# An attention and MLP kernel on one core: the second tile of x loaded from SP's queue, and head 0's wq issued behind the activation table load

## The chip, the cores and the metric

The kernel runs on one core of one Trainium2 chip. The metric is the device time of one execution in microseconds (us). The time of an execution is about 1.8 us more than the span of its profile (1238.05 against 1236.3 us in the profiled execution of the kernel before). A ratio of two kernels is the mean time of one kernel's fast runs over that of the other's of the same rounds, so it is not quite the ratio of the medians quoted.

## The reference

```python
x  = A_x                                   # 1 x 2048 x 512, bf16
xn = layernorm(x)
q  = (xn @ wq) as 32 heads of 128
p  = softmax(q @ k_cache^T / sqrt(128))    # 2048 keys a head
s  = (p @ v_cache) @ wo
h  = relu(xn @ w1 + b1) ** 2
g  = silu(h @ w2 + b2)
out = x + s * g
```

## The kernel before

Five engines run their own instruction lists; a helper adds the semaphore waits. TensorE (PE) takes its list strictly in order. The list begins with 36 warm-up matmuls on zeros. Head 0 has a start of its own: its keys come in two halves by plain loads, are transposed on PE and copied to SBUF by ACT, while the first tile of x is normalized on DVE and POOL, transposed on PE, copied by DVE and projected with head 0's wq.

The loads, as they stand in the program before:

```python
ln_load(0, 0, SP)          # x tile 0, 128 rows of 1 KB
ln_load(0, 1, AC)          # x tile 1
load_k0(0)                 # first half of head 0's keys, 128 rows of 2 KB, on SP
fill_wq(0, AC)             # head 0's wq, 512 rows of 256 B
load_k0(1)                 # second half of the keys, on SP
E(AC, partial(_act, out=th_t[:, 0, 0:1], in_=warm[:, 0:1], func=ACT.Exp), deps=[t_warm])
ln_load(0, 2, SP)
ln_load(0, 3, SP)
fill_wq(1)                 # head 1's wq, on SP
load_v0(0)
load_v0(1)
# ... cut: head 1's keys and values, w1
```

The order in which PE gets its first work:

```python
warm_up(36)
k0_transpose(0)            # PE: 8 transposes of the first keys
k0_copy(0)                 # ACT
ln_bn(0, 0)                # DVE: statistics of x tile 0
ln_rstd(0, 0, eng=DV)
ln_bn(0, 1)
ln_scale(0, 0)
first_transpose(0)         # PE: 4 transposes of x tile 0
k0_transpose(1)            # PE: 8 transposes of the second keys
k0_copy(1)                 # ACT
t_kfill[0] = t_k0[1]
ln_rstd(0, 1, eng=DV)
first_copy(0)              # DVE
first_proj(0)              # PE: first projection, needs wq
bias_rows()                # PE
ln_scale(0, 1)
first_evac(0)
bias_copy()
first_transpose(1)         # PE
gen_scores(0)              # PE, and exp on ACT
# ... cut
```

The transposes of the second keys stand before the first projection.

The softmax here doesn't subtract the row's maximum and nothing guards it: scores larger than these inputs give would overflow.

## Time and profile before

| kernel before | value |
|---|---|
| time, median of 6 runs | 1237.94 us (1237.75 to 1238.45) |
| span of the profiled execution | 1236.3 us |
| PE busy | 1231.7 us |
| ACT, DVE, POOL busy | 1053.5, 472.8, 31.9 us |
| first keys landed | 5.20 us |
| second keys landed | 1.67 + 4.3 = 6.0 us (issue and time to landing in the DMA view) |
| first projection on PE | 7.02 us |

PE is busy almost throughout, and the prediction shows why only the first 8 us are open to this change. The start in the view of the chain that ended last, where each line is a start, a duration in us and what took it:

```profile
1.18 4.02 DMA kT<-in_A_k_cache_dram
5.20 0.05 issue
5.24 0.94 PE psO L196 x8
6.19 0.24 PE psF L196 x4
...
7.02 0.38 PE psF L152 x4
```

The chain enters PE with the landing of the first keys at 5.20. `PE psO L196 x8` are eight key transposes, `PE psF L196 x4` the four x transposes, and `PE psF L152 x4` is the first projection.

### The profile page before, as it was taken

Reading aid. Unit: us, or ns where it says so; the run is one execution under the profiler, and the core shown is the slowest. Engines: PE = TensorE matmul, PEld = TensorE weight load, DVE = VectorE, ACT = ScalarE, POOL = GpSimd, SP = SyncE. Lnnn points to the kernel's source line nnn. Section 1 sums busy time; section 2 is a strip of 40 time slices with the busy share of each in tenths; the row PEclk is TensorE's granted clock in tenths of the full one; section 3 lists DMA queues with packets and bytes.
Section 4 is the critical chain, followed back from the end, with each engine's and each line's share of the span. In section 5 each row is a group of like instructions: output and inputs, shape, how many; then the busy total and the mean of one; then the engine's idle time right before and its main releaser. Section 6 shows DMA issues by size and latency. Waiting matters only on the chain.

```text
span 1236.3 us, 26934 instructions
## 1 busy us (share of the span) xinstructions
PE 1231.7 (100%) x11885; PEld 818.8 (66%) x11885; DVE 472.8 (38%) x953; ACT 1053.5 (85%) x1044; POOL 31.9 (3%) x73
## 2 busy tenths in 40 slices
PE   9999999999999999999999999999999999999999
PEld 7666666666666666666666666666666666666665
DVE  4453323244435332334444532333344333324333
ACT  7888888888888888888888888888888888888885
POOL 1010000000002000000000200000000000000000
PEclk9999999999999999999999999999999999999999
DMA  9999998777879897778778878787788789878771
GB/s 211 203 231 209 185 178 134 130 144 143 139 152 172 141 161 129 139 139 145 133 133 170 172 138 143 141 148 134 133 146 148 146 154 158 137 134 146 145 123 31
DMA packets 686868, 185.41 MB, mean 150 GB/s; under 512 B 673536, under 2 KB 685568, under 8 KB 686752
## 3 DMA queue, kind: packets, MB, share of 16 engines
q1 hardware_dynamic: 684656, 179.62, 80.4%
q0 software_dynamic: 1424, 3.81, 1.2%
q8 instruction: 94, 1.54, 0.6%
q10 hardware_dynamic: 672, 0.26, 0.1%
q14 instruction: 22, 0.18, 0.1%
HBM read 96.60 MB, written 2.10 MB: 80 GB/s over the span
## 4 chain that ended last, share of the span: by engine, by line
PE 99%; DMA 0%; DVE 0%; issue 0%; SPq 0%; DVEq 0%
PE psO L157 38%; PE psA L152 36%; PE psF L152 25%; DMA kT<-in_A_k_cache_dram 0%; PE psA L157 0%; DVE out_t L165 0%; PE psF L196 0%; DVE tmp_t L175 0%; PE psO L196 0%; PE psO L152 0%; DVE xnT L179 0%; SPq L208 0%; PE psA L196 0%; DVEq L119 0%
## 5 line engine op out<-in xcount | busy, mean ns | idle before, releaser
L161 ACT ACTIVATE pT<-psA 128x1024 bf16<-128x1024 f32 x1024 | 1043.5, 1023 | 163.5 <-PE psA L152 118.1
L157 PEld LDWEIGHTS psO<-v_sb,pT 128*128 128x128 bf16 x8192 | 547.7, 98 | 240.5 <-issue 12.5
L157 PE MATMUL psO<-v_sb,pT 128*128 128x129 bf16 x8192 | 631.6, 220 | 0.0
L152 PE MATMUL psA<-qt_sb,kT 128*128 128x512 bf16 x2032 | 604.8, 379 | 0.0
L179 DVE COPY o_un<-psO 128x258 f32<-128x258 f32 x256 | 97.4, 422 | 399.4 <-PE psO L157 398.7
L152 PE MATMUL psF<-xnT,wq_sb 128*128 128x512 bf16 (+1 forms) x520 | 168.9, 374 | 0.2 <-DVE xnT L179 0.2
L152 PE MATMUL psF<-wo_all,oT 128*128 128x512 bf16 x480 | 163.8, 379 | 0.0
L152 PEld LDWEIGHTS psA<-qt_sb,kT 128*128 128x128 bf16 x2032 | 156.9, 98 | 0.0
L179 DVE CAST qt_sb<-psF 128x512 bf16<-128x512 f32 (+1 forms) x130 | 88.0, 677 | 97.4 <-PE psF L152 97.4
L165 DVE TENSOR_TENSOR o_bf<-o_un,rden 128x512 bf16<-128x512 f32 x128 | 88.6, 692 | 4.7 <-DVE rden L183 0.3
L152 PEld LDWEIGHTS psF<-xnT,wq_sb 128*128 128x128 bf16 x520 | 50.2, 98 | 60.1 <-issue 0.3
L171 DVE TENSOR_SCALAR r_t<-psF,b1f 128x512 bf16<-128x512 f32 x56 | 42.0, 750 | 117.5 <-PE psF L152 117.5
L152 PEld LDWEIGHTS psF<-wo_all,oT 128*128 128x128 bf16 x480 | 46.9, 98 | 56.4
L152 PE MATMUL psF<-xnT,w_sb 128*128 128x512 bf16 x224 | 77.1, 379 | 0.0
L152 PE MATMUL psF<-w_sb,h2T 128*128 128x512 bf16 x224 | 74.2, 379 | 0.0
L152 PEld LDWEIGHTS psF<-xnT,w_sb 128*128 128x128 bf16 x224 | 21.9, 98 | 26.5
L152 PEld LDWEIGHTS psF<-w_sb,h2T 128*128 128x128 bf16 x224 | 21.9, 98 | 26.5
L165 DVE TENSOR_TENSOR z_t<-psF,b2bc 128x512 f32<-128x512 f32 x16 | 11.1, 692 | 67.2 <-PE psF L152 67.2
L165 DVE TENSOR_TENSOR acc<-psF,acc 128x512 f32<-128x512 f32 x28 | 19.3, 689 | 29.9 <-PE psF L152 29.9
L208 POOL DMA_DIRECT2D out_dram<-out_t x12 | 6.7, 554 | 891.0 <-DVE out_t L165 891.0
L165 DVE TENSOR_TENSOR h2T<-r_t 128x512 bf16<-128x512 bf16 x56 | 23.8, 425 | 1.9
L183 DVE RECIPROCAL rden<-o_un 128x4 f32<-128x4 f32 x128 | 22.9, 179 | 4.4
(47 smaller groups left out, 165.6 us busy)
## 6 DMA issues: line engine op xcount, KB each, us to landing
v_sb<-in_A_v_cache_dram SPq DMA_DIRECT2D x127, 512.0 KB, 4.7
wq_sb<-in_A_wq_dram SPq DMA_DIRECT2D x127, 128.0 KB, 3.1
wo_all<-in_A_wo_dram SPq DMA_DIRECT2D x4, 1024.0 KB, 6.7
w_sb<-in_B_w_dram SPq DMA_DIRECT2D x14, 256.0 KB, 4.3
oT<-o_bf SPq DMA_TRANSPOSE x128, 4.0
x_t<-in_A_x_dram POOLq DMA_DIRECT2D x16, 128.0 KB, 3.4
kT<-in_A_k_cache_dram SPq DMA_TRANSPOSE x127, 4.5
x_ln<-in_A_x_dram SPq DMA_DIRECT2D x15, 128.0 KB, 3.8
```

What stands on the lines that cost most here:

```text
L152: return e.matmul(out, lhsT, rhs, start=start, stop=stop)
L157: return e.matmul(out, lhsT, rhs, start=start, stop=stop, skip_group_check=True)
L161: return e.activation(out, in_, func, bias=bias, scale=scale)
L165: return e.tensor_tensor(out, in0, in1, op)
L171: return e.tensor_scalar(out, in0, scalar1=scalar1, scalar2=scalar2, op0=op0, op1=op1)
L179: return e.tensor_copy(out, in_)
L183: return e.reciprocal(out, in_)
L208: return e.dma_start(out, in_)
```

## The change

The intent is to let the loads of x and of the keys go through one queue in the order in which they are needed, and to let ACT load its activation table at once, before it issues head 0's wq.

```diff
     ln_load(0, 0, SP)
-    ln_load(0, 1, AC)
+    ln_load(0, 1, SP)
     load_k0(0)
-    fill_wq(0, AC)
     load_k0(1)
     E(AC, partial(_act, out=th_t[:, 0, 0:1], in_=warm[:, 0:1], func=ACT.Exp), deps=[t_warm])
+    fill_wq(0, AC)
     ln_load(0, 2, SP)
```

The order of instructions on PE, DVE and POOL is the same in both kernels.

## The prediction

> **What bounds the kernel now.** I read the page first, then the list of waits of PE, then the chain of waits and the timeline of the first 20 us, because the change touches only the first few instructions. The page:
>
> ```profile
> PE 1231.7 (100%) x11885; PEld 818.8 (66%) x11885; DVE 472.8 (38%) x953; ACT 1053.5 (85%) x1044; POOL 31.9 (3%) x73
> ...
> PE 99%; DMA 0%; DVE 0%; issue 0%; SPq 0%; DVEq 0%
> ```
>
> TensorE (PE) is busy in 1231.7 of 1236.3 us, and the chain that ended last lies on it for 99% of the span. The 4.6 us in which it isn't busy are the only time that another order of loads can give back. The waits of PE over the whole execution say where a load is behind them:
>
> ```profile
> PE psA L152 <- POOL mhalf L187: 1.0, 1, 1.0
> PE psO L196 <- DMA kT<-in_A_k_cache_dram: 0.2, 1, 0.2
> PE psF L152 <- DVE xnT L179: 0.2, 1, 0.2
> ```
>
> The first 1.0 us is the start of the program. The one wait for a transfer is 0.2 us, for the first half of head 0's keys (kT). Most of the rest is the tail: the table of windows gives PE 13.26 us of the last 17 (1220 to 1237), and the diff doesn't touch the tail. From 8 us on PE waits for nothing that the list shows, so whatever the start gains or loses should reach the end one for one. The start in order of time:
>
> ```profile
> 0.72 0.40 ACTq L208 DMA_DIRECT2D x_ln<-in_A_x_dram  x1
> 0.73 0.40 SPq L208 DMA_DIRECT2D x_ln<-in_A_x_dram  x1
> 0.98 3.76 PEld L152 LDWEIGHTS psA<-warm 128*128 128x128 bf16 x36 [0.98 <-POOL mhalf L187]
> 1.15 0.45 ACTq L208 DMA_DIRECT2D wq_sb<-in_A_wq_dram  x1
> 1.18 1.00 SPq L208 DMA_DIRECT2D kT<-in_A_k_cache_dram  x2
> 1.63 1.28 ACT L161 ACT_TABLE_LOAD   x1 [1.63 <-PEq L1025]
> 2.93 0.21 ACT L161 ACTIVATE th_t<-warm 128x1 bf16<-128x1 bf16 x1
> 3.71 0.69 DVE L200 BATCH_NORM_STATS2 st_t<-x_ln 128x6 f32<-128x512 bf16 x1 [3.71 <-DMA x_ln<-in_A_x_dram]
> 5.24 0.77 PEld L196 LDWEIGHTS psO<-ident,kT 128*128 128x128 bf16 x8 [0.51 <-DMA kT<-in_A_k_cache_dram]
> 5.50 0.41 DVE L171 TENSOR_SCALAR xn_t<-x_ln,mv_t,rstd 128x512 bf16<-128x512 bf16 x1
> 5.97 0.27 PEld L196 LDWEIGHTS psF<-ident,xn_t 128*128 128x128 bf16 x4
> 7.02 0.38 PE L152 MATMUL psF<-xnT,wq_sb 128*128 128x128 bf16 x4 [0.16 <-DVE xnT L179]
> ```
>
> Two paths meet at 5.97, where the first normalized x tile is transposed: the keys (issued 1.18, landed 5.20, eight key transposes from 5.24) and x (landed 3.71, normalized by 5.91). They are nearly tied. The weight loads of the warm-up end at 0.98 + 3.76 = 4.74, so PE's weight path stands idle 0.51 us before the first key transpose; the 0.2 us of the list is shorter only because matmul ends are modelled. So 0.5 us is about the most that earlier keys can give.
>
> **What the Trainium skill says.** "DMA: Bandwidth & Descriptors", section "Issuing engines are not separate DMA queues": transfers of all issuers run on the same 16 DMA engines and interleave; a second issuer saves only sequencer time. The trace agrees: x tile 1 from ACT and x tile 0 from SP were issued 0.01 us apart and landed 2.7 and 3.0 us later, the tile that is needed first being the later one; and from 2.5 to 5.2 us the ACT queue took 29.5% and the SP queue 72.4% of the 16 engines. So head 0's wq, which PE wants only at 7.02, takes transfer time from the keys wanted at 4.74. "ScalarE: Activation LUTs", section "What ACT_TABLE_LOAD costs": about 1283 ns for the load and about 1380 ns of drain. The trace has 1.28 us, and the ACTIVATE starts 0.02 us after it, so no such drain is seen here. "Perfetto Trace Analysis", section "Sequencer Loop": the sequencer pushes an engine's instruction into a queue and goes on to the next, so the wq issue need not wait for the table load before it. No line of the trace of before shows that order, so I work out both cases. "TensorE: Matmul & The Clock Gate", section "What's actually happening": PE starts at half clock and is released by a free-running activity window of about 3.4 us. The trace agrees in kind: eight key transposes took 0.94 us at 5.24 and the second eight 0.61 us at 6.25. A gain before that release buys work at the slow rate.
>
> **The change part by part.**
> Issue. x tile 1 moves from ACT to SP behind tile 0. SP issues one x tile in 0.40 to 0.46 us, so every later SP issue comes about 0.43 us later: first keys at 1.6 instead of 1.18. ACT loses one issue (0.40 us), so its table load starts at about 0.72 instead of 1.63. The issue of wq then comes at about 0.8 to 1.0 (sequencer runs on) or about 2.2 (it waits: 0.72 + 1.28 + 0.21), against 1.15. ACT is next wanted at 6.23, so the table load itself is off the path either way. Instructions added or removed: none; the order of PE, DVE and POOL is the same.
>
> x path. Tile 0 no longer shares its transfer with tile 1. A tile is 128 KB, about 0.4 us at the 320 GB/s that the DMA view shows from 2.5 to 5.2 us. I estimate a landing 0.4 to 0.8 us earlier, near 3.1. The chain on DVE and POOL (3.71 to 5.91, 2.2 us, with tile 1's statistics inside it) then ends near 5.3. Tile 1 lands at some 3.6 and is wanted after 4.1, so it doesn't hold DVE up.
>
> Keys. Before, x0, x1, wq and the keys share the engines: 128 + 128 + 128 + 256 = 640 KB, 2.0 us at 320 GB/s from the 2.5 us at which the transfers run full, plus some 0.5 us until seen: 5.0, against the measured 5.20. After, with wq late, 512 KB lie ahead: 1.6 us, so 4.6 from the same start; the issue 0.43 us later takes part of it only if the queue runs dry, which an issue rate of 128 KB in 0.43 us (300 GB/s) makes unlikely. With wq early they share as before, but tile 0 starts sooner. I estimate 4.3 to 4.9. PE is then held by its own warm-up until 4.75: the first key transpose comes at 4.75 to 4.95 instead of 5.24, a gain of 0.3 to 0.5 us.
>
> Then to the path. Eight key transposes take 0.77 us of weight loads: the x transposes can start near 5.55 to 5.7 (xn_t is there at 5.3) instead of 5.97. If the clock is released at the same time as before, about 6.0 to 6.2, all four run slow, which costs about 0.05 us. The copy (0.43) and the first projection follow at about 6.6 to 6.7 instead of 7.02.
>
> wq. It must be there by 6.6. Early case: landed by about 5.4. Late case: 2.2 + 4.2 (its landing before) = 6.4, just in time. After that, values of head 0 (landing at about 3.64 + 5.0 = 8.6, first used at 9.68) have a volume ahead of them that hasn't changed, so they should land at 8.6 to 9.0 against a new need of 9.3.
>
> Sum: keys -0.4, slow clock +0.05, the rest 0: about -0.35 us, so 1237.87 - 0.35 = 1237.5 us, or 0.03%.
>
> **The rivals.**
> 1. wq replaces the keys as the wait. For it: in the late case the margin is 0.2 us, and its transfer takes turns with the second keys and x tiles 2 and 3. Against it: before, it landed at 5.35, 1.7 us ahead of need, and the volume ahead of it doesn't grow. It would cost up to 0.8 us, with a time of 1237.9 to 1238.3.
> 2. The issue order holds the keys: SP's 0.43 us reach the landing in full, at 5.2 to 5.6. For it: the keys were issued at 1.18 and landed after 4.0 us, much of it latency. Against it: the engines were full from 2.5 on, so the queue and not the issue set the landing. Time 1237.9 to 1238.3.
> 3. The clock release moves. The window runs free, so an execution in which the release falls a microsecond later loses about half of that, whatever the order of loads. The three runs of before spread over 0.7 us (1237.75 to 1238.44), as much as any effect above.
> 4. A gain above 0.5 us: only if PE's later order loosens as well. PE is busy 5.00 of 5.00 us from 12 to 17, and ACT 4.01, which speaks against it.
>
> **Range and chances.** The effect is -0.5 to +0.5 us and the median of three runs moves by some 0.3 us; chips and sessions may differ by a little more. Predicted 1237.5 us, range 1236.8 to 1238.3. Two per cent is 24.8 us, five times all of PE's idle time, so only a slow execution or a broken start could reach it: faster 0.003, same 0.994, slower 0.003.
>
> **What would show it.** Right: the first statistics on DVE start near 3.1 instead of 3.71; the weight-load gap before the first key transpose falls from 0.51 to under 0.25; the first projection starts near 6.6; PE from 12 us on is unchanged, and its busy time stays at 1231 to 1232 us. Whether the wq issue stands at about 0.9 or at 2.2 tells what ACT's sequencer does. Wrong: a wait of the first projection for wq (rival 1), keys landing at 5.2 or later (rival 2), or a start that gains while the time doesn't (rival 3, or a wait on values after 9 us).

## The result and the profile after

The changed kernel takes 1238.72 us (median of 6 runs, 1238.53 to 1239.87) against 1237.94 us. The ratio is 1.0007 with a 95% interval from 0.9994 to 1.0019: the same by the 2% measure, and by the interval not told from no change. The two sets of runs don't overlap, though: its fastest run is slower than the slowest of the kernel before. The same happened when it ran again (below). So it is slower by about 0.8 us, where the prediction had it faster by 0.4, and 1238.72 lies above the range. This holds for runs of the same rounds: in the later groups the kernel before reached 1238.46, and once 1239.76.

The page of the changed kernel, busy time and chain:

```profile
PE 1220.4 (99%) x11678; PEld 819.0 (66%) x11885; DVE 472.7 (38%) x953; ACT 1054.6 (85%) x1044; POOL 32.0 (3%) x73
...
PE 98%; issue 1%; DMA 0%; DVE 0%; SPq 0%; DVEq 0%
```

The lower PE busy time is no saving: 11678 of 11885 matmul records are in this trace, the weight loads (PEld) are all there and take 819.0 us, against 818.8 before. The waits of PE over the whole execution are (total, times, longest, in us):

```profile
PE psO L196 <- DMA kT<-in_A_k_cache_dram: 1.4, 1, 1.4
PE psA L152 <- POOL mhalf L187: 1.0, 1, 1.0
```

The wait for keys has grown from 0.2 to 1.4 us. The timeline says which keys:

```profile
0.72 1.28 ACT L161 ACT_TABLE_LOAD   x1 [0.72 <-PEq L1025]
0.72 0.87 SPq L208 DMA_DIRECT2D x_ln<-in_A_x_dram  x2
...
0.96 0.42 ACTq L208 DMA_DIRECT2D wq_sb<-in_A_wq_dram  x1
...
1.65 0.90 SPq L208 DMA_DIRECT2D kT<-in_A_k_cache_dram  x2
...
2.93 0.69 DVE L200 BATCH_NORM_STATS2 st_t<-x_ln 128x6 f32<-128x512 bf16 x1 [2.93 <-DMA x_ln<-in_A_x_dram]
...
4.89 0.49 PEld L196 LDWEIGHTS psO<-ident,kT 128*128 128x128 bf16 x8 [0.16 <-DMA kT<-in_A_k_cache_dram]
...
7.21 0.45 PEld L196 LDWEIGHTS psO<-ident,kT 128*128 128x128 bf16 x8 [1.61 <-DMA kT<-in_A_k_cache_dram]
7.62 0.27 PEld L152 LDWEIGHTS psF<-xnT,wq_sb 128*128 128x128 bf16 x4
```

The first keys and x tile 0 came earlier, as meant: x at 2.93 instead of 3.71, the first key transposes at 4.89 instead of 5.24. Then PE stands before the second eight key transposes until 7.21, and the first projection behind them starts at 7.67 (its matmul) instead of 7.02, although x was transposed and copied by 6.24 and wq had landed at 0.96 + 2.8 = 3.8 us. The chain gives the landing of the second keys:

```profile
2.11 5.06 DMA kT<-in_A_k_cache_dram
7.17 0.05 issue
7.22 0.62 PE psO L196 x8
```

So the second keys were issued 0.44 us later than before (2.11 against 1.67), but landed 1.2 us later (7.17 against 6.0). The loss at the first projection, 0.65 us, is nearly the whole loss of the profiled span, 1237.0 - 1236.3 = 0.7 us. The view of windows shows the transfers themselves; in each row the last two numbers are the busy share of the 16 DMA engines (it can come out above 1) and GB/s. Before:

```profile
4.00:5.00 1.00, 1.00 (x10) 0.73 (x7) 0.93 (x4) 0.00 (x0) 0.10 (x1) 1.00 1.02 311
5.00:6.00 1.00, 0.76 (x9) 0.76 (x9) 0.91 (x3) 0.00 (x0) 0.47 (x1) 1.00 1.10 352
```

After:

```profile
4.00:5.00 1.00, 1.00 (x12) 0.84 (x10) 0.88 (x3) 0.00 (x0) 0.57 (x1) 1.00 0.70 176
5.00:6.00 1.00, 0.78 (x13) 0.60 (x11) 0.59 (x4) 0.41 (x1) 0.48 (x1) 1.00 0.83 236
```

In the two microseconds in which the second keys should move, the engines moved 412 KB instead of 663 KB. What had gone ahead is in the DMA view of the changed kernel from 2.5 to 3.0 us (queue, packets, MB, share of the 16 engines; q10 is ACT's queue with wq, q1 is SP's):

```profile
q10 hardware_dynamic: 380, 0.10, 83.9%
q1 hardware_dynamic: 20, 0.02, 10.1%
```

### The profile page after: what moved, and what is told of

Its sections match the earlier page's. It is cut to its first block, busy times and chain, and to the rows that moved or that the text cites. A ratio compares the mean times of both kernels' runs of the same rounds, so it can differ in the third digit from the quotient of the medians.

```text
span 1237.0 us, 26727 instructions
## 1 busy us (share of the span) xinstructions
PE 1220.4 (99%) x11678; PEld 819.0 (66%) x11885; DVE 472.7 (38%) x953; ACT 1054.6 (85%) x1044; POOL 32.0 (3%) x73
## 4 chain that ended last, share of the span: by engine, by line
PE 98%; issue 1%; DMA 0%; DVE 0%; SPq 0%; DVEq 0%
PE psO L157 38%; PE psA L152 35%; PE psF L152 25%; DMA kT<-in_A_k_cache_dram 0%; PE psA L157 0%; DVE out_t L165 0%; SPq L208 0%; DVE tmp_t L175 0%; PE psF L196 0%; PE psO L152 0%; PE psO L196 0%; DVE xnT L179 0%; PE psA L196 0%; DVEq L119 0%
## 5 line engine op out<-in xcount | busy, mean ns | idle before, releaser
L152 PE MATMUL psA<-qt_sb,kT 128*128 128x512 bf16 x1840 | 562.9, 379 | 10.1
L152 PE MATMUL psF<-xnT,wq_sb 128*128 128x512 bf16 (+1 forms) x508 | 165.7, 374 | 0.3
```

The costliest lines, as they stand in the source:

```text
L152: return e.matmul(out, lhsT, rhs, start=start, stop=stop)
```

## The experiments

In the theory, the second keys land late and PE, in order, turns that into a late first projection, after which nothing changes. The table gathers the start in each profiled execution: landings, the time that the first eight key transposes took (it hints at the TensorE clock then), the first projection, the span, their difference, and the timed runs.

| kernel | first keys | second keys | 8 transposes | first projection | span | span - projection | time, median (range) |
|---|---|---|---|---|---|---|---|
| before | 5.20 | 6.0 | 0.94 | 7.02 | 1236.3 | 1229.3 | 1237.94 (1237.75-1238.45) |
| before_again | 4.4 | 6.1 | 1.06 | 6.92 | 1236.2 | 1229.3 | 1237.96 (one run) |
| changed | 4.9 | 7.17 | 0.66 | 7.67 | 1237.0 | 1229.3 | 1238.72 (1238.53-1239.87) |
| after_again | 5.1 | 7.35 | 0.62 | 8.22 | 1238.1 | 1229.9 | 1238.98 (1238.51-1239.95) |
| x1_sp_only | 5.32 | 6.2 | 0.82 | 7.02 | 1236.3 | 1229.3 | 1238.37 (1238.05-1238.54) |
| table_first_only | 4.7 | 6.22 | 0.62 | 6.73 | 1236.0 | 1229.3 | 1237.97 (1237.73-1238.21) |
| k0b_act | 6.92 | 6.8 | 0.62 | 8.42 | 1238.6 | 1230.2 | 1240.40 (1240.25-1240.82) |
| wq_late | 4.6 | 5.7 | 0.72 | 6.35 | 1235.6 | 1229.3 | 1237.89 (1237.42-1238.54) |
| one_queue | 4.6 | 5.2 | 0.62 | 6.44 | 1235.7 | 1229.3 | 1237.52 (1237.37-1237.60) |
| one_queue_again | 4.5 | 5.4 | 1.06 | 6.89 | 1236.2 | 1229.3 | 1237.81 (1237.53-1238.21) |
| wq1_act | 6.10 | 6.9 | 0.62 | 7.59 | 1236.9 | 1229.3 | 1239.30 (1238.63-1240.00) |
| pe_order | 4.8 | 7.2 | 0.63 | 6.30 | 1236.7 | 1230.4 | 1238.56 (1238.50-1238.85) |
| x2_act | 4.9 | 5.9 | 1.03 | 7.06 | 1236.3 | 1229.2 | 1238.22 (1237.87-1238.67) |
| wq_mid | 5.14 | 6.6 | 1.03 | 7.21 | 1236.5 | 1229.3 | 1238.19 (1238.12-1238.25) |
| x1_act_late | 4.3 | 6.27 | 1.06 | 6.80 | 1236.1 | 1229.3 | 1237.94 (1237.72-1238.67) |
| b1_sp | 5.0 | 7.0 | 0.62 | 7.52 | 1237.0 | 1229.5 | 1238.85 (1238.83-1238.94) |
| b1_act | 4.8 | 5.4 | 0.91 | 6.56 | 1235.8 | 1229.2 | 1237.91 (1237.64-1237.98) |

Landings are issue plus time to landing where the chain or the timeline doesn't give them directly. The kernel before, run beside these, had medians of 1238.05, 1238.08, 1238.16, 1237.82 and 1237.78 us in the five groups (after_again to k0b_act; wq_late to pe_order; x2_act, wq_mid and one_queue_again; x1_act_late; b1_sp, b1_act and before_again).

The column of differences is the first finding. Over a spread of 1.3 us in the first projection (6.35 to 7.67) the rest takes 1229.2 to 1229.3 us. The exceptions have a reason each: a slow clock after the first projection (after_again, k0b_act), a wait after it (b1_sp for the bias load, pe_order for the copy of the second keys). So in these profiles a change of the loads is worth what it does to the start, and no more.

### The changed kernel again

No edit.

> The changed kernel unaltered, for a second profile. Theory (the second half of head 0's keys lands late because only one DMA queue has work then, and PE, which takes instructions in order, stands before its transposes): the late landing repeats, at 6.8 to 7.5 us, PE waits 1.2 to 1.7 us for it, first scores at 8.4 to 8.9 us against 7.96 in the kernel before, time +0.5 to +1.0 us. Rival (single key packets stalled by chance in the one profiled execution): the landing falls back to about 6 us and the first scores to about 7.5, and the median comes out at 1237.5.

The late landing repeats (7.35), and the rival of chance is out: 1.0008 (0.9993 to 1.0023), the four runs again all above the kernel before in the same rounds (1237.73 to 1238.34). This execution shows something more. Its windows, where the third number from the right is the granted TensorE clock:

```profile
7.00:8.00 1.00, 0.60 (x6) 0.61 (x7) 0.00 (x0) 0.00 (x0) 0.00 (x0) 0.53 1.28 283
8.00:9.00 1.00, 1.00 (x12) 0.78 (x10) 0.11 (x1) 0.53 (x1) 0.00 (x0) 0.50 1.14 196
```

PE had waited twice for keys, 2.1 us in all, and from 7 to about 10.5 us the clock stood at half: the eight second key transposes took 1.03 us instead of 0.62. The span is 1.1 us longer than in the first profile of the same kernel. I read the outlying runs of the changed kernel near 1239.9 us in this way; for the one whose mean clock lies below 1 (1239.87 us, clock 0.999, span 1238.1) it fits, for others it is an inference. The run of the kernel before at 1239.76 us has a clock of 1.000, so it isn't explained in this way.

### The two parts alone

```diff
 # x1_sp_only, against the changed kernel
-    E(AC, partial(_act, ... func=ACT.Exp), deps=[t_warm])
     fill_wq(0, AC)
+    E(AC, partial(_act, ... func=ACT.Exp), deps=[t_warm])
```

> One part of the change alone: x tile 1 on SP, while ACT issues wq before its table load, as in the kernel before. Theory: wq is issued 0.2 us earlier than in the changed kernel and nothing else differs, so it behaves as the changed kernel: second keys at 6.8 to 7.5 us, time +0.5 to +1.0 us. Rival (the order of table load and wq matters): as the kernel before, +0.0.

```diff
 # table_first_only, against the changed kernel
-    ln_load(0, 1, SP)
+    ln_load(0, 1, AC)
```

> The other part alone: x tile 1 stays on ACT and the table load and the exp come between it and wq. The sequencer ran past the table load in the changed kernel, so wq is issued at about 1.2 us as in the kernel before. Theory: as the kernel before, keys landing at 5.2 and 6.0 us, time within 0.2 us of it. Rival (the table load holds wq back): wq issued at 2.6 us or later and the first projection waits for it, +0.5 us or more.

The table load in front of wq costs nothing: wq was issued at 1.23 us, 0.06 us after the table load began, and the time is 0.9999 (0.9984 to 1.0014) of the kernel before. The move of x tile 1 alone came out between its two expectations: 1.0002 (0.9987 to 1.0017), four runs from 1238.05 to 1238.54, and the profiled one, the fastest of the four, had its second keys at 6.2 and its first projection where the kernel before has it. So neither part alone showed the loss that both together have. And wq was first in the ACT queue here too, issued at 0.73 us instead of 0.96, yet the second keys landed 1 us earlier than in the changed kernel: wq ahead of them doesn't always cost so much, and no run here tells why.

### The second keys on the other queue

```diff
-    load_k0(1)
     E(AC, partial(_act, ... func=ACT.Exp), deps=[t_warm])
     fill_wq(0, AC)
+    load_k0(1, AC)
```

> The changed kernel with the second half of the keys issued from ACT behind wq, so that both queues have work from 2 to 5 us. Theory: it is issued at about 1.4 us, takes turns with the first half, both land by 5.6 us, PE's wait for the second half vanishes (under 0.2 us), the first scores start at 7.4 to 7.6 us and the time is 0.3 to 0.6 us below the kernel before. Rival (the volume ahead or the memory sets the landing, not the number of queues): the first half lands later by what the second half takes, at 5.3 us or more, and the time is at best that of the kernel before.

A miss, and a clear one: 1.0019 (1.0003 to 1.0036), the only interval here that leaves out 1. The halves shared the transfers and both were late (6.92 and 6.8 us):

```profile
1.64 5.27 DMA kT<-in_A_k_cache_dram
6.92 0.05 issue
6.96 0.62 PE psO L196 x8
```

The first half, which PE needs at 4.7, landed at 6.92. The second half was in fact issued first, at 1.45 us from ACT against 1.64 from SP. The second queue wasn't more room here; it let a later need share with an earlier one.

### wq held back, and wq behind the keys

```diff
 # wq_late
-    E(AC, partial(_act, ... func=ACT.Exp), deps=[t_warm])
+    t_e = E(AC, partial(_act, ... func=ACT.Exp), deps=[t_warm])
+    S.emit_wait(AC, [t_e])
     fill_wq(0, AC)
```

> The changed kernel with wq held back until the exp of ACT has ended, so that it is issued at about 2.25 us instead of 0.97 and moves while the keys move, not before them. Theory A (the second keys are late because wq is already through when they move, so that only one queue has work): the second keys land at 5.6 to 6.2 us, PE's wait for them is under 0.3 us, first projection at 6.4 to 6.9 us, time 0.2 to 0.5 us below the kernel before. Rival B (x tile 1 on SP makes the key issue 0.47 us later, and that alone makes the landing late): landing at 6.8 us or more again, time +0.5 us or more.

```diff
 # one_queue
-    fill_wq(0, AC)
+    fill_wq(0, SP)
```

> The changed kernel with wq on SP behind both halves of the keys: nothing on the ACT queue, and 128 KB less ahead of the keys. Theory A (one queue alone drains slowly while the keys move): the second keys land at 6.5 us or more although less lies ahead of them, and the time is +0.3 us or more. Rival C (only the volume ahead counts): the second keys land at 5.3 us or before, PE doesn't wait for them, time 0.2 to 0.5 us below the kernel before.

These two take wq out of the way of the keys, one in time, the other by order. In wq_late wq is issued at 2.25 us; the chain of its start:

```profile
5.00 0.52 PE psO L196 x8
...
5.78 0.62 PE psO L196 x8
6.40 0.34 PE psF L152 x4
```

In one_queue the timeline of PE has:

```profile
4.66 0.62 PE L196 MATMUL psO<-ident,kT 128*128 128x128 bf16 x8
...
5.36 0.61 PE L196 MATMUL psO<-ident,kT 128*128 128x128 bf16 x8
...
6.44 0.40 PE L152 MATMUL psF<-xnT,wq_sb 128*128 128x128 bf16 x4 [0.47 <-DVE xn_t L171]
```

In both the second keys land at 5.2 to 5.7 us, the wait for them is gone, and PE gets to the first projection 1.2 to 1.3 us earlier than in the changed kernel, and 0.2 us earlier than the prediction had it. Rival B falls: x tile 1 is on SP and the keys are issued at 1.65 and 2.1 us in both, as in the changed kernel. Theory A, that one queue alone drains slowly, falls with one_queue, which has nothing at all on the ACT queue and the earliest second keys (though its transfer engines, too, were busy for only 0.78 and 0.80 of the time from 4 to 5 and 5 to 6 us). In one_queue it is now wq that lands last, at 2.60 + 3.8 = 6.4 us. (The line above names a DVE instruction as what PE waited for, but the program has no such dependence: that instruction merely ended just then, and the view of wq_sb puts 0.6 us of PE's wait down to wq.) Its times are 0.9995 (0.9980 to 1.0010) of the kernel before; wq_late is at 0.9998 (0.9983 to 1.0013).

### More on the second queue

```diff
 # wq1_act
     fill_wq(0, AC)
+    fill_wq(1, AC)
     ln_load(0, 2, SP)
     ln_load(0, 3, SP)
-    fill_wq(1)
```

> The changed kernel with head 1's wq issued from ACT right behind head 0's, at about 1.4 us: 128 KB more beside the keys, on the second queue. Theory A: the second queue has work until about 4.5 us, and the second keys land earlier than the 7.17 and 7.35 us of the changed kernel, by 0.5 us or more, although more is ahead of them. Rival C (volume): they land later, at 7.3 us or more, time +0.8 us or more.

The second keys came at 6.9, between the two expectations, but neither had seen that the first keys would be pushed to 6.10 us, and these now set the start. The time went to 1239.30 us, 1.0011 (0.9995 to 1.0028). So another 128 KB on the ACT queue beside the keys was no help to the start.

### PE's order

```diff
 # pe_order
     first_transpose(0)
-    k0_transpose(1)
-    k0_copy(1)
-    t_kfill[0] = t_k0[1]
     ln_rstd(0, 1, eng=DV)
     ...
     first_transpose(1)
+    k0_transpose(1)
+    k0_copy(1)
+    t_kfill[0] = t_k0[1]
     gen_scores(0)
```

> The changed kernel with the transfers as they are and the eight transposes of the second keys moved on PE behind the first projection, the bias transpose and the transpose of x tile 1. The keys land at about 7.2 us as before. Theory (PE in order turns a late landing into a late projection): the first projection starts at 6.3 to 6.6 us instead of 7.67, PE's wait for the keys falls from 1.4 to about 0.3 us, and the time is 0.2 to 0.5 us below that of the changed kernel; not below the kernel before, because the second scores still need these keys copied. Rival (PE's order is of no account): no change of the time.

With the transfers as in the changed kernel (second keys at 7.2), the first projection starts at 6.30 instead of 7.67. This shows that only PE's order held it back: x, wq and the copy were ready. The wait moves on rather than away; the waits of PE now have:

```profile
PE psA L157 <- ACT kT L161: 0.7, 1, 0.7
PE psF L152 <- DVE xnT L179: 0.6, 1, 0.6
```

The second scores wait for ACT's copy of the late keys until 8.98. The span is 0.3 us below the first profile of the changed kernel and the median 0.16 us below its first, just short of the 0.2 us expected; 1.0004 (0.9989 to 1.0019) against the kernel before.

### What about wq delays the keys

```diff
 # x2_act
     E(AC, partial(_act, ... func=ACT.Exp), deps=[t_warm])
-    fill_wq(0, AC)
-    ln_load(0, 2, SP)
+    ln_load(0, 2, AC)
+    fill_wq(0)
```

> The changed kernel with x tile 2 in wq's place on ACT (issued at about 0.97 us) and wq on SP behind the keys: the same 128 KB go ahead of the keys on the second queue, but as 128 rows of 1 KB instead of 512 rows of 256 B. Theory C (the volume ahead of the keys counts): the second keys land as late as in the changed kernel, at 6.8 us or more, and the time is +0.4 us or more. Theory D (the 512 short rows of wq count[...]): the second keys land at 5.8 us or before, PE doesn't wait for them, and the time is at or below the kernel before; the first projection may then wait for wq until about 6.5 us.

The same 128 KB in the same place, as 128 rows of 1 KB instead of 512 of 256 B: the second keys land at 5.9 us, 1.3 us earlier than behind wq and some 0.6 us later than with nothing there. Both theories are too simple; in this comparison, of one profile, something other than volume counts for more. The row size is the likely thing, but the two loads also read different arrays, x in one piece and wq with a large step between its rows, and no run separates these. The time is 1.0001 (0.9985 to 1.0018). The first eight transposes took 1.03 us in this execution, which hid the earlier keys.

```diff
 # wq_mid
     load_k0(0)
+    fill_wq(0)
     load_k0(1)
     E(AC, partial(_act, ... func=ACT.Exp), deps=[t_warm])
-    fill_wq(0, AC)
```

> All on SP in the order x0, x1, first keys, wq, second keys, x2, x3. In the kernel with wq behind both key halves the second keys landed at 5.3 us and the first projection waited for wq until 6.44. Theory C (volume in front sets each landing): wq lands at about 5.3 and the second keys at 5.6 to 5.9 us, the first projection starts at 6.1 to 6.4, and the time is 1237.2 to 1237.5. Theory D or a slow stretch of the transfers between 4 and 6.5 us whatever is in it: the second keys fall into that stretch and land at 6.3 us or later, and the time is at or above that of the kernel before.

wq between the halves on one queue: second keys at 6.6, 1.0000 (0.9984 to 1.0017). They were issued 0.48 us later than in one_queue, and wq's 128 KB at the 320 GB/s of the prediction are another 0.4 us; the landing is 1.2 to 1.4 us later. So in this one profile, too, wq ahead cost the keys 0.3 to 0.5 us more than its volume, and here without a second queue.

### One queue again

No edit against one_queue.

> The kernel with wq on SP behind the keys, unaltered, to see whether it beats both kernels again: 1237.4 to 1237.7 us in every execution, 0.4 to 0.7 us below the kernel before, second keys landing at 5.1 to 5.5 us. If the first result was luck of one chip: within 0.2 us of the kernel before.

The landings repeat (4.5 and 5.4), the time less so: 1237.53 to 1238.21 us, 0.9998 (0.9983 to 1.0013). The profiled execution shows where the rest went:

```profile
4.79 1.06 PE L196 MATMUL psO<-ident,kT 128*128 128x128 bf16 x8
...
6.89 0.39 PE L152 MATMUL psF<-xnT,wq_sb 128*128 128x128 bf16 x4
```

The same eight transposes took 1.06 us instead of 0.62, and the first projection started 0.45 us later with its data there. I take it for the slow TensorE clock of the start, because the same transposes take 0.62 us elsewhere, and took 1.03 us in after_again where the granted clock reads 0.53; the granted clock in the table of windows reads 1.00 in this stretch and doesn't show it, as it doesn't for the warm-up, so this is read from the durations alone. So one_queue beats the changed kernel (all its eight runs lie below the fastest of that kernel's ten, though they were not run in the same rounds), but against the kernel before its gain of 0.3 to 0.6 us in the means isn't clear of this noise.

### A version meant to beat both

```diff
 # x1_act_late
     ln_load(0, 0, SP)
-    ln_load(0, 1, SP)
     load_k0(0)
     load_k0(1)
     E(AC, partial(_act, ... func=ACT.Exp), deps=[t_warm])
-    fill_wq(0, AC)
+    ln_load(0, 1, AC)
+    fill_wq(0)
```

> A version meant to beat both kernels: SP issues x0, both key halves, wq, x2, x3; ACT loads its table and then issues x tile 1. The keys keep the issue times of the kernel before (1.18 and 1.6 us), wq stands behind them, and the tile on the other queue has 128 rows of 1 KB. If what comes ahead of the second keys sets the start: second keys land by 5.3 us, wq by 6.1, the first projection starts at 6.0 to 6.5 us (7.02 in the kernel before, 7.67 in the changed one), and since the end follows the first projection by 1229.3 us in the profiles so far, the time is 1237.1 to 1237.6 us. If a second queue beside the keys is harmful as such, the keys land no earlier than in the kernel before and the time is 1237.9 or more.

A miss: 1.0000 (0.9986 to 1.0014). The first keys came at 4.3, the earliest of all, but the second took 4.62 us to land, at 6.27, although they were issued as early as in the kernel before and nothing with short rows was ahead of them. So the landing of the second keys isn't told by what is ahead alone.

### The small load of b1, and the kernel before again

```diff
 # b1_sp, against the changed kernel; b1_act has it on ACT, against one_queue
-tok_b1 = S.emit_dma(GP, partial(_dma, out=b1b[:], ...), sl_b1)
 ...
     fill_wq(1)
+    tok_b1 = S.emit_dma(SP, partial(_dma, out=b1b[:], ...), sl_b1)
     load_v0(0)
```

> The changed kernel with the small load of b1 (14 rows of 256 B) moved from POOL, whose descriptors reach the transfer engines at about 4 to 6 us, to SP behind head 1's wq. Theory E (the POOL load is what slows the second keys between 4 and 6.5 us): they land at 5.3 to 6.0 us instead of 7.2, PE doesn't wait for them, time 0.2 to 0.5 us below the kernel before. If wq ahead of the keys on the ACT queue is what counts (theory F): landing again at 6.8 us or more and time +0.5 us or more.

> The kernel with wq on SP behind the keys, and the small load of b1 (3.5 KB) on ACT at 0.97 us instead of POOL: the ACT queue has something ahead of the keys, but almost no volume. Theory F1 (any transfer on the ACT queue ahead of the keys delays them, however small): second keys at 5.9 us or later instead of 5.2 to 5.4, time as the kernel before or above. Theory F2 (what is ahead counts by its size and rows): second keys at 5.1 to 5.5 us as without it, first projection at 6.3 to 6.9, time 1237.4 to 1237.9.

> The kernel before, unaltered, for a second profile of its start: keys at 5.0 to 5.4 and 5.8 to 6.3 us, first projection at 6.6 to 7.2 us, span minus first projection 1229.3 us. If its landings move by more than that, the differences of 0.5 us among the other profiles can't be read.

The POOL load is not the cause: without it the second keys still land at 7.0 us, and the time is 1.0009 (0.9994 to 1.0024). Nor is just anything on the ACT queue: with the 3.5 KB there they land at 5.4 us, as in one_queue, at 1.0001 (0.9984 to 1.0018). The second profile of the kernel before (a single run, state unknown) has its second keys at 6.1 after 6.0, while the first keys moved from 5.20 to 4.4, outside the expected range. By the test set before that run, differences of 0.5 us among single profiles can't be read from landings that move so. The second keys repeat better within a kernel (6.0 and 6.1; 7.17 and 7.35; 5.2 and 5.4), so the steps of 1 us and more between the kernels stand.

## Why the prediction was wrong

- **What bounds the kernel**, and that the start reaches the end one for one: right. The rest took 1229.3 us after the first projection in nearly every profile.
- **Issue**: right, in the early case. The keys were issued at 1.65 us, and wq at 0.96 while the table load ran to 2.00.
- **x path**: right, a little better than told. x landed at 2.93 (predicted near 3.1), and the normalized tile was there at 5.16 (predicted near 5.3).
- **Keys**: right for the first half, 4.9 us in the range of 4.3 to 4.9, and the gap before the transposes fell to 0.16 us.
- **Then to the path** is the step that failed, and with it the "rest 0" of the sum. It said: "The copy (0.43) and the first projection follow at about 6.6 to 6.7 instead of 7.02." It left out that the transposes of the second keys stand on PE between the x transposes and the first projection, and so the landing of the second keys was nowhere worked out. It was 7.17 us, PE waited 1.44 us for it, and the projection started at 7.67. With pe_order, which only takes these transposes out of the way, it started at 6.30: the omitted term is the whole error at this point.
- **wq** was judged for its own landing alone. It landed at 3.8 us, where the prediction had 5.4 in the early case. It was early because it went through ahead of the keys, as the DMA view from 2.5 to 3.0 us shows. Holding it back (wq_late) or putting it behind them (one_queue) gives second keys at 5.2 to 5.7 and, in the first profile of each, a first projection at 6.35 to 6.44.
- **Slow clock**: predicted 0.05 us. In the first profile of the changed kernel it didn't occur: its eight transposes took 0.66 us from 4.90, nearly the 0.62 of full speed. Between the two profiles of one_queue a difference of 0.45 us is put down to it, so from one execution to the next it can be larger than the predicted gain, as rival 3 said. In the changed kernel the clock fell back to half after the wait in one profiled execution, whose span was 1.1 us longer.
- **The sum**: 7.67 + 1229.3 + 1.8 = 1238.8 us, against 1238.75 in the profiled run. With the 6.65 of the prediction it would have been 1237.75; the other 0.2 us of the error lies mostly in taking the gain off the median of three runs (1237.87) instead of the profiled run of 1238.05. The "0.5 us until seen" in the sum for the keys has no source in the traces.
- **Rivals**: rival 2, a key landing that takes the place of the one removed, came closest, but for the wrong half and in spite of an earlier first half. Rival 1, wq as the wait, didn't occur in the changed kernel.

What stays open: why the second keys lose up to 2 us to a load of 128 KB. In one_queue they are issued as late as in the changed kernel, at 2.1 us, and land at 5.2 or 5.4; wq's volume ahead (0.4 us) would give 5.6 to 5.8, and 7.0 to 7.35 was seen in the four profiles that have wq on ACT at 0.96 us and nothing else there. The low share of the transfer engines from 4 to 6 us (0.70 and 0.83) doesn't tell the kernels apart: one_queue moved only 240 + 218 = 458 KB in the same stretch, with its keys in time. What the changed kernel has is a long tail. The key rows are the only packets of 2 KB in this stretch, and the DMA views from 4 to 5, 5 to 6 and 6 to 7 us count 76, 54 and 16 of them, while packets of loads issued after the keys already move. The other three such profiles have 13 to 20 from 6 to 7; one_queue has 81 from 4 to 5 and none later. So a part of the key rows falls behind, and the last of them sets the landing. It isn't the POOL load, it isn't the mere use of the ACT queue, and it isn't that one queue has the work alone. x1_act_late and x1_sp_only show that row size isn't all of it either.

## What to carry to other kernels

List for an in-order engine everything that stands before the instruction of interest, and give each its own landing; the last one sets the time, not the one that the profile of before shows as a wait. A load that is moved to another queue isn't out of the way: here 128 KB issued 0.7 us ahead of a more urgent load went with a landing 1.6 to 2.2 us later (7.0 to 7.35 against 5.2 and 5.4), while with them behind it, or held back, it landed at 5.2 to 5.7. One profile with wq ahead, x1_sp_only, had 6.2, so the size of the loss is not a constant. And where a change is worth half a microsecond, a start that depends on the clock's release needs several profiles of the same kernel before two kernels are compared.

## What the Trainium skill lacked or had wrong

- "DMA: Bandwidth & Descriptors", section "Issuing engines are not separate DMA queues", tells that transfers interleave, and elsewhere on the page it is told that the engines take turns between queues, but not what that does to a later transfer on another queue: with head 0's wq on ACT at 0.96 us, ahead of them, the second keys landed at 7.0 to 7.35 us; with it on SP behind them, at 5.2 and 5.4.
- "ScalarE: Activation LUTs", section "What ACT_TABLE_LOAD costs", adds about 1.38 us of drain to the load. At the start of these kernels the load took 1.28 us and the ACTIVATE began 0.02 us after it, with nothing before it to drain.
- The pages on DMA say that short rows are slow in themselves, but none says whether the row size of a load ahead matters to a load behind it: 128 KB in 128 rows left the second keys at 5.9 us (one profile), 128 KB in 512 rows at 7.0 to 7.35 (four), but at 6.2 when issued 0.23 us earlier (x1_sp_only, one).
